# Four token tiles normalised on VectorE: a float32 transformer block on one Trainium2 core

## The chip, the core and the metric

The kernel runs on one core of a Trainium2 chip. The core has a matrix engine, TensorE (PE in the profile, with its weight loads as PEld), and three engines for everything else: VectorE (DVE), ScalarE (ACT) and GpSimd (POOL). SyncE (SP) issues the transfers between the chip's memory and the on-chip memory SBUF. Matmul results land in a second on-chip memory, PSUM. Each engine takes its instructions strictly in the order in which the program gives them, and waits at the first whose inputs are not ready. The metric is the device time of one execution in microseconds.

## The reference

One block of a transformer with two parallel branches on the same normalised input; 2048 tokens, width 576, all in float32:

```python
x = A_x
xn = _layernorm(x, axis=-1)          # (x - mean) / sqrt(var + 1e-5), over the 576 columns
return x + _A_ref(xn, A_wqkv, A_wo) + _B_ref(xn, B_w1, B_b1, B_w2)
```

`_A_ref` is attention with 32 heads of 18, where each token sees 8 earlier tokens at a distance of 2 from each other; `_B_ref` is a dense layer to 4608, the Mish function, and a dense layer back.

## The kernel before, in words

The tokens are worked through in two halves of 1024 (`hf` 0 and 1), each of two blocks of 512 (`b`), each of four tiles of 128 tokens (`jj`). A float32 number is split for TensorE into a high part, rounded to the format fp32r, and the low rest; a product is the sum of three matmuls (high by high, high by low, low by high). So every weight tile `wq_k` has a high half, made by a ScalarE cast, and a low half, made by a subtraction of the cast from the raw tile.

The program is one long list of items in the order of TensorE's work, and around each of them the code places the work of the other engines. The order on each engine is that of the code; a manual dependency on the instruction before fixes it. The list begins with `first_item(0)` to `first_item(3)`: the first group of query, key and value columns for the four tiles of the first block. `first_item(0)` runs `prologue()`, which normalises tiles 0 and 1. During the item of tile n, `mid()` is called between two of its 14 matmuls and transposes tile n + 1.

One tile goes through these steps:

- The load `acc_0_n` (SyncE, L59). The first tile, two weight tiles, the second tile and three weight tiles are loaded first; `hold` keeps the later loads back until the first tile's statistics are taken.
- `ln_stats`: two BN_STATS over 288 columns each (L114) and a BN_AGGR (L115) on VectorE give mean and variance, the two columns of `mv`.
- `ln_root`: VectorE adds epsilon to the variance (`ve`, L160), and ScalarE takes the inverse root by a logarithm and an exponential (`rs`, L161 and L162).
- `ln_newton`: VectorE makes the root exact with a Newton step (L169 to L171), and for ScalarE's use also computes `nm`, the negative product of mean and root (L172). Tiles 0 to 3 are each a group of their own (`k == 1`); tiles 4 and 5, and 6 and 7, are handled in pairs by the other branch.
- `ln_norm`: ScalarE writes `xn`, the tile times `rs` plus `nm` (L182), and GpSimd copies its last 64 columns once more behind it (L183).
- `ln_transpose`: GpSimd sets the rest aside (`rem`, L194); TensorE transposes the tile into the PSUM tiles `ta` and `tb` (L77, L78); ScalarE casts these to the high part of `xt` (L83 for `ta`, L88 for `tb`), and VectorE subtracts to get the low part (L84 for `ta`, L89 for `tb`). The matmuls of `qkv_item` (L349) read `xt` as their stationary operand.

`first_cast` makes the first five weight tiles: the high half on ScalarE at once (L1172), the low half (L1173, here always on GpSimd) when the function that it returns is called.

The core of `mid()` and its place among the matmuls, in short:

```python
if n == 0: ln_root(2); ln_newton(2)
ln_transpose(0, 0, n + 1)
if n == 0: ln_norm(2); ln_stats(3); ln_root(3); ln_newton(3)
if n == 1: ln_norm(3)
```

It stands before the twelfth matmul of tile 0, the ninth of tile 1 and the fifth of tile 2.

Of the kernel before, what the change touches and what calls it, by code (L numbers as in the profile page):

```python
# [10 lines left out]
AF = mybir.ActivationFunctionType  # L11
ALU = mybir.AluOpType
AX = mybir.AxisListType.X

S, D, F = 2048, 576, 4608
# [24 lines left out]
def block_kernel(ctx: ExitStack, tc: tile.TileContext, x, wq, wo, w1, b1, w2, mask, out):  # L40
    nc = tc.nc
# [11 lines left out]
    def load_x(hf, blocks=range(NB), jjs=range(JB)):  # L53
        tiles = []
        xv = x[hf * SH:(hf + 1) * SH, :].rearrange("(p j) d -> p j d", j=TJ)
        for b in blocks:
            for jj in jjs:
                t = sb.tile([P, D], F32, tag="acc", bufs=9, name=f"acc_{hf}_{b}_{jj}")
                nc.sync.dma_start(t, xv[:, b * JB + jj, :])  # L59
                tiles.append(t)  # L60
        return tiles
# [7 lines left out]
    def transpose_split(src, dst, col, extra=None, pair=False):  # L69
        n = next(tpn)  # L70
        if pair:
            ta, tb = (ps.tile([P, 512], F32, tag="out", bufs=4, name=f"tt{k}_{n}") for k in range(2))
        else:
            ta = ps.tile([P, 512], F32, tag="h", bufs=4, name=f"ta_{n}")
            tb = ps.tile([P, 512], F32, tag="h", bufs=4, name=f"tb_{n}")
        for k in range(KT):
            nc.tensor.transpose(ta[:, k * P:(k + 1) * P], src[:, k * P:(k + 1) * P], ident)  # L77
        nc.tensor.transpose(tb[:, 0:P], src[:, KT * P:(KT + 1) * P], ident)  # L78
        if extra is not None:
            nc.tensor.transpose(tb[:, P:2 * P], extra, ident)  # L80
        tav = ta.rearrange("p (k t) -> p k t", k=KT)
        hi = dst[:, 0:KT, col:col + P]
        nc.scalar.copy(hi, tav)  # L83
        nc.vector.tensor_sub(dst[:, 5:5 + KT, col:col + P], tav, hi.bitcast(F32))  # L84
        e = 1 if extra is None else 2
        hr = dst[:, KT:KT + 5 * e - 4:5, col:col + P]
        tbv = tb.rearrange("p (k t) -> p k t", k=KT)[:, 0:e]
        nc.scalar.copy(hr, tbv)  # L88
        nc.vector.tensor_sub(hr[64:P], tbv[64:P], hr[64:P].bitcast(F32))  # L89
# [20 lines left out]
    def stats(n, t, mv):  # L110
        st = odd.tile([P, 2, 6], F32, tag="st", bufs=4, name=f"st_{next(tpn)}")
        last = None
        for c in range(2):
            last = nc.vector.bn_stats(st[:, c, :], t[:, c * 288:(c + 1) * 288])  # L114
        nc.vector.bn_aggr(mv, st)  # L115
        return last

    def newton(rs, ve, y, eng=nc.vector):
        eng.tensor_mul(y, rs, rs)
        eng.tensor_mul(y, y, ve)  # L120
        eng.tensor_scalar(y, y, -0.5, 1.5, op0=ALU.mult, op1=ALU.add)
        eng.tensor_mul(rs, rs, y)
# [23 lines left out]
    def ln_group(ns):  # L146
        k = len(ns)
        mk_ = lambda w, c: odd.tile([P, 4, c], F32, tag=w, bufs=3, name=f"{w}_{ns[0]}")
        g = dict(n0=ns[0], k=k, mv=mk_("mv", 2), ve=mk_("ve", 1), rs=mk_("rs", 1), y=mk_("y2", 1), nm=mk_("nm", 1))
        for n in ns:  # L150
            group[n] = g

    def ln_stats(n):
        g = group[n]
        return stats(n, accs[0][n], g["mv"][:, n - g["n0"], :])

    def ln_root(n0):
        g = group[n0]
        k, rs, ve = g["k"], g["rs"][:, 0:g["k"]], g["ve"][:, 0:g["k"]]
        nc.vector.tensor_scalar_add(ve, g["mv"][:, 0:k, 1:2], EPS)  # L160
        nc.scalar.activation(rs, ve, AF.Ln)  # L161
        nc.scalar.activation(rs, rs, AF.Exp, scale=-0.5)  # L162

    def ln_newton(n0):
        g = group[n0]
        k, rs, ve, y, nm = g["k"], *(g[w][:, 0:g["k"]] for w in ("rs", "ve", "y", "nm"))
        if k == 1:
            r, v, y, m = rs[:, 0], ve[:, 0], y[:, 0], nm[:, 0]
            nc.vector.tensor_scalar(y, r, r, v, op0=ALU.mult, op1=ALU.mult)  # L169
            nc.vector.tensor_scalar(y, y, -0.5, 1.5, op0=ALU.mult, op1=ALU.add)  # L170
            nc.vector.tensor_scalar(r, r, y, None, op0=ALU.mult)  # L171
            nc.vector.tensor_scalar(m, g["mv"][:, 0, 0:1], r, -1.0, op0=ALU.mult, op1=ALU.mult)  # L172
        else:
            newton(rs, ve, y)
            nc.vector.tensor_mul(nm, g["mv"][:, 0:k, 0:1], rs)
            nc.vector.tensor_scalar(nm, nm, -1.0, None, op0=ALU.mult)

    def ln_norm(n):
        g = group[n]
        i = n - g["n0"]  # L180
        xn = sb.tile([P, 5 * P], F32, tag="xn", bufs=XNB, name=f"xn_0_{n}")
        nc.scalar.activation(xn[:, 0:D], accs[0][n], AF.Identity, bias=g["nm"][:, i, :], scale=g["rs"][:, i, :])  # L182
        nc.gpsimd.tensor_copy(xn[:, D:D + 64], xn[:, KT * P:D])  # L183
        xns[0, n] = xn

    def ln_transpose(hf, b, jj):
        if jj == 0:
            XTs[hf, b] = sb.tile([P, 9 + b, TB], F32R, tag=f"xt{b}", bufs=1, name=f"xt_{hf}_{b}")
        xn = xns[hf, b * JB + jj]
        if (b, jj) == (0, 0):  # L190
            rems[hf] = sb.tile([P, JB, P], F32, tag="tt", bufs=2, name=f"rem_{hf}")
        rem = rems[hf][:, jj, :]
        if b == 0:
            nc.gpsimd.tensor_copy(rem, xn[:, KT * P:])  # L194
        else:
            nc.gpsimd.tensor_tensor(out=rem, in0=rem, in1=xn[:, KT * P:], op=ALU.subtract)
        transpose_split(xn, XTs[hf, b], jj * P, rem if b else None, (hf, b) == (1, 0) and jj < 3)
# [21 lines left out]
    def new(kind, hf, i):  # L219
        tag, bufs, width = home(kind, i)  # L220
        return sb.tile([P, 2, width], F32R, tag=tag, bufs=bufs, name=f"{kind}_{hf}_{i}")
# [879 lines left out]
    accs = {0: load_x(0, [0], [0])}  # L1101
# [6 lines left out]
    def hold(ins):  # L1108
        tiles = load_x(0, [0], [2, 3])
        first = nc.cur_bb.bb.instructions[-len(tiles)]  # L1110
        tc.add_manual_dep(first, ins.ins.name,
                          mybir.DependencyInfo(mybir.DependencyClass.Sync, mybir.DependencyReason.DATA),
                          reason="the other tiles' loads begin behind the first tile's")
        for k in range(4):
            load("wq", 5 + k)
        accs[0].extend(tiles + load_x(0, [1]))
        rest_loads()
# [52 lines left out]
    def first_cast(k, eng):  # L1170
        t = done["wq", 0, k] = new("wq", 0, k)
        nc.scalar.copy(t[:, 0, :], rq0[k])  # L1172
        return lambda: eng.tensor_tensor(out=t[:, 1, :], in0=rq0[k], in1=t[:, 0, :].bitcast(F32),  # L1173
                                         op=ALU.subtract)

    def prologue():
        for ns in ((0,), (1,), (2,), (3,), (4, 5), (6, 7)):
            ln_group(ns)
        hold(ln_stats(0))
        ln_root(0)  # L1180
        first_cast(0, nc.gpsimd)()
        ln_newton(0)
        ln_stats(1)
        low1 = first_cast(1, nc.gpsimd)
        ln_norm(0)
        low1()
        first_cast(2, nc.gpsimd)()
        ln_root(1)
        ln_newton(1)
        ln_transpose(0, 0, 0)  # L1190
        first_cast(3, nc.gpsimd)()
        ln_norm(1)
        first_cast(4, nc.gpsimd)()
        ln_stats(2)

# [137 lines left out]
    def spot(hf, q, i):  # L1333
        return at["s", hf, q, i]

    for q in range(NP):
        if q == 0:
            i = at["q", 0, 3, 1, 0]
            ps_ = dict(raw=i - 3, sums=i - 1, wa=i, wc=i + 1, t0=i + 2, t1=i + 4)
        elif q == 1:  # L1340
            i = at["q", 0, 3, 0, 0]
# [16 lines left out]
    for q in range(1, 2 * OC + 1):  # L1358
        i = spot(0, q, (3,2)[q > 1])
# [5 lines left out]
    i = spot(0, NP - 1, 0)  # L1365
# [5 lines left out]
    i = at["q", 1, 0, 1, 1]  # L1371
# [4 lines left out]
    i = spot(0, 9, 4)  # L1376
# [10 lines left out]
    for q in range(NP):  # L1387
        if q == 0:
            i = at["z", JB - 1, 0]
            ps_ = dict(wa=i - 7, t0=i - 6, t1=i - 5, wc=i - 4)  # L1390
        elif q == 1:
            i = spot(1, 0, 0)
# [19 lines left out]
    for n, (a, b) in enumerate((("P6", "P1"), ("P7", "P6"), ("P6", "P5"), ("P2", "P1"), ("P3", "P6"), ("P4", "P7"), ("P5", "P7"))):  # L1412
        for pr in range(2):
            i = items[-2][2] + 1 + (0,1,2)[n] if n < 3 else at["p", 1, J + 0 - 1, n > 4, pr] + (1, 7, 1, 2)[n - 3]
# [6 lines left out]
    i = at["q", 0, 1, 1, 0]  # L1421
# [3 lines left out]
    i = at["q", 0, 3, 1, 0]  # L1425
# [5 lines left out]
    i = at["q", 1, 0, 1, 1]  # L1431
    for n in range(8):
        c, k = divmod(n, 4)
# [7 lines left out]
    for n in range(0, JB, 2):  # L1441
        i = at["q", 0, 1, 0, n]
# [4 lines left out]
    for n in range(TJ):  # L1447
        i = spot(0, 2 + n, 2)
# [3 lines left out]
    i = spot(0, NP - 2, 0)  # L1452
# [7 lines left out]
    for n, (name, pr) in enumerate((name, pr) for name in ("P4", "P5", "P2", "P3") for pr in range(2)):  # L1460
        i = items[dict(P4=0, P5=2, P3=2, P2=3)[name]][2] + pr
# [29 lines left out]
    k = marks[0] - 1  # L1491
    for n in range(2 * steps):
        t = n * total / (2 * steps)
        if n == steps:
            k = max(k, spot(1, 0, 0) + 1)
        k = next(k for k in range(k + 1, len(plan)) if T[k + 1] > t and ok[k])
# [6 lines left out]
    i = spot(1, *(11,3))  # L1503
# [4 lines left out]
    for n, name in enumerate(("T3", "T1", "T2", "T4", "B11", "B21", "B22", "R", "D")):  # L1508
        k = i + 10 + (0,5,10,15,20,25,30,35,40)[n]
# [5 lines left out]
    i = spot(1, NP - 1, 0)  # L1515
# [68 lines left out]
```

## Time and profile before

| | before |
|---|---|
| median of 3 runs | 1124.03 us (1123.45 to 1124.14) |
| span of the profiled execution | 1121.6 us |
| PE busy | 1109.5 us (99%) |
| VectorE busy | 829.0 us (74%) |
| ScalarE busy | 492.1 us (44%) |
| GpSimd busy | 787.7 us (70%) |

The span goes from the first instruction to the last on the core; the time of a run also has what lies around it. For the profiled execution the profile gives the span alone, 1121.6 us, which is 2.4 us below the median of the runs. A share of busy time is an average over all stages: the stretch that the change touches is the first 20 us.

### The profile page before, as it was taken

What the parts mean: (1) busy time and instruction counts of PE and PEld (TensorE: products, weight loads), DVE (VectorE), ACT (ScalarE), POOL (GpSimd) and SP (SyncE); (2) the same over time, 40 slices, a digit from 0 to 9 for tenths busy, and PEclk for the clock granted to TensorE, in tenths of its full rate; (3) what the DMA queues carried; (4) which work ended last, traced back from release to release, by engine and by line L of the source; (5) the groups of instructions that cost most, each with busy time, mean ns of one, the idle gap of its engine ahead of it and who ended that gap; (6) DMA issues with size and microseconds to landing.
All of it is one profiled execution on the core that took longest, in us unless ns stands there. A gap on an engine that the chain in (4) does not pass through costs nothing.

```text
span 1121.6 us, 18415 instructions
## 1 busy us (share of the span) xinstructions
PE 1109.5 (99%) x6630; PEld 1023.0 (91%) x6630; DVE 829.0 (74%) x1351; ACT 492.1 (44%) x892; POOL 787.7 (70%) x639
## 2 busy tenths in 40 slices
PE   8999999999999999999999999999999999999998
PEld 7999899999999999899999889999999999999998
DVE  6368788888888888877655456687866677776876
ACT  5544645544554545455233355343433343443332
POOL 2488767767689687676788476665789878668632
PEclk9999999999999999999999999999999999999999
DMA  6899885868767849666596797655655477676463
GB/s 200 283 312 318 290 283 205 289 228 284 261 240 258 282 163 345 222 240 214 191 342 238 231 373 249 241 200 174 227 198 189 168 263 269 215 253 248 157 222 104
DMA packets 147487, 271.08 MB, mean 242 GB/s; under 512 B 30114, under 2 KB 86724, under 8 KB 147396
## 3 DMA queue, kind: packets, MB, share of 16 engines
q1 hardware_dynamic: 147396, 269.91, 69.2%
q8 instruction: 52, 0.85, 0.3%
q14 instruction: 39, 0.32, 0.1%
HBM read 160.39 MB, written 109.48 MB: 241 GB/s over the span
## 4 chain that ended last, share of the span: by engine, by line
PE 89%; DVE 4%; POOL 3%; DMA 2%; issue 1%; ACT 1%; DVEq 0%; POOLq 0%; SPq 0%
PE h L657 28%; PE po L755 19%; PE pq L349 11%; PE po L868 10%; PE po L847 7%; PE h L663 5%; PE o L1056 4%; PE z L447 2%; DMA acc<-in_x 1%; POOL accP L856 1%; DVE u L801 1%; POOL pr L534 0%; DVE accP L871 0%; POOL act L709 0%; DMA z_B<-kept_wq 0%
## 5 line engine op out<-in xcount | busy, mean ns | idle before, releaser
L755 PEld LDWEIGHTS po<-w,act 128*128 128x128 f32 x1728 | 236.4, 188 | 7.5 <-DVE acc L759 1.7
L755 PE MATMUL po<-w,act 128*128 128x288 f32 x1728 | 240.8, 295 | 1.4 <-DVE acc L759 1.2
L534 POOL TENSOR_TENSOR pr<-q,kv 128x576 f32<-128x576 f32 x128 | 195.7, 1553 | 18.7 <-DMA q<-q_d 16.9
L572 POOL TENSOR_TENSOR pv<-L,kv 128x576 f32<-128x576 f32 x128 | 174.3, 1461 | 38.7 <-DVE L L565 20.9
L709 POOL TENSOR_TENSOR act<-c,act 128x512 fp32r<-128x512 f32 x81 | 107.1, 1322 | 128.4 <-ACT act L708 125.5
L759 DVE TENSOR_TENSOR acc<-po,acc 128x288 f32<-128x288 f32 x288 | 120.4, 450 | 31.6 <-PE po L755 30.2
L349 PE MATMUL pq<-wq,xt 128*128 128x432 f32 x672 | 136.2, 361 | 1.8 <-ACT xt L83 1.8
L868 PEld LDWEIGHTS po<-w,act 128*128 128x128 f32 x960 | 131.1, 188 | 3.7 <-DVE accP L871 0.4
L868 PE MATMUL po<-w,act 128*128 128x288 f32 x960 | 133.8, 295 | 0.2
L349 PEld LDWEIGHTS pq<-wq,xt 128*128 128x128 f32 x672 | 125.0, 188 | 8.7 <-ACT xt L83 2.7
L703 ACT ACTIVATE c<-c,b1c 128x512 f32<-128x512 f32 x81 | 58.7, 724 | 132.9 <-DVE c L702 132.6
L657 PE MATMUL h<-xt,t 128*128 128x512 f32 x432 | 110.6, 391 | 0.9 <-DVE c L702 0.8
L657 PE MATMUL h<-S,t 128*128 128x512 f32 x432 | 110.4, 391 | 0.0
L691 ACT COPY c<-h 128x512 f32<-128x512 f32 x81 | 47.4, 586 | 136.5 <-PE h L663 78.3
L578 DVE TENSOR_REDUCE og<-pv 128x144 f32<-128x1152 f32 x64 | 85.9, 1343 | 25.4 <-POOL pv L572 25.4
L657 PE MATMUL h<-xt,wa 128*128 128x512 f32 x432 | 104.0, 390 | 0.0
L657 PEld LDWEIGHTS h<-xt,wa 128*128 128x128 f32 x432 | 80.9, 188 | 16.9
L871 DVE TENSOR_TENSOR accP<-po,accP 128x288 f32<-128x288 f32 x160 | 69.6, 454 | 36.1 <-PE po L868 34.5
L847 PEld LDWEIGHTS po<-pw,u 128*128 128x128 f32 x672 | 92.4, 188 | 2.9 <-DVE u L801 0.5
L847 PE MATMUL po<-pw,u 128*128 128x288 f32 x672 | 94.2, 296 | 0.3 <-DVE u L801 0.3
L539 DVE TENSOR_REDUCE L<-pr 128x64 f32<-128x1152 f32 x64 | 85.8, 1341 | 11.2 <-POOL pr L534 11.1
L657 PEld LDWEIGHTS h<-xt,t 128*128 128x128 f32 x432 | 79.0, 188 | 16.1 <-DVE c L702 1.1
(231 smaller groups left out, 1840.5 us busy)
## 6 DMA issues: line engine op xcount, KB each, us to landing
kv<-kv_d SPq DMA_DIRECT2D x64, 396.0 KB, 5.2
kept_t<-t SPq DMA_DIRECT2D x36, 512.0 KB, 5.3
t<-kept_t SPq DMA_DIRECT2D x36, 512.0 KB, 5.4
rw<-in_w SPq DMA_DIRECT2D x36, 320.0 KB, 4.6
kept_wa<-wa SPq DMA_DIRECT2D x18, 640.0 KB, 3.5
kept_w<-w SPq DMA_DIRECT2D x20, 576.0 KB, 4.8
wa<-kept_wa SPq DMA_DIRECT2D x18, 640.0 KB, 6.1
w<-kept_w SPq DMA_DIRECT2D x20, 576.0 KB, 4.5
```

The lines of the kernel that those rows point to most:

```text
L349: nc.tensor.matmul(pq[:, 0:432], XT[:, xi, tok], wt[wi][:, hl, 0:432], start=i == 0, stop=i == len(seq) - 1)
L534: nc.gpsimd.tensor_tensor(out=pr[:, x:x + hh], in0=q[:, j0 + x:j0 + x + hh, None, :].to_broadcast([P, hh, W, CU]), in1=win(kt, 0, CU, j0 + ...
L539: nc.vector.tensor_reduce(L[:, k, j0:j0 + hj].rearrange("p j w h -> p (j w h)"), pr.rearrange("p j w (h d) -> p (j w h) d", h=2), axis=AX, ...
L572: nc.gpsimd.tensor_tensor(out=pr[:, x:x + hj].rearrange("p j d w -> p j w d"), in0=L[:, k, x:x + hj, :, h:h + 1].to_broadcast([P, hj, W, DH]),
L578: nc.vector.tensor_reduce(og[:, :, c0:c0 + DH], pr, axis=AX, op=ALU.add)
L657: nc.tensor.matmul(ph, wt[:, wl, wk * P:(wk + 1) * P], X[:, xs, :], start=first and i == 0, stop=last and i == len(seq) - 1, skip_group_ch ...
L709: nc.gpsimd.tensor_tensor(out=a[:, 1, :], in0=t, in1=a[:, 0, :].bitcast(F32), op=ALU.subtract)
L755: nc.tensor.matmul(po, acts[hf, q, b, j][:, al, tok], done["w2", hf, 2 * q + j][:, wl, c * HC:(c + 1) * HC], start=i == 0, stop=i == 5)
L759: nc.vector.tensor_tensor(out=t, in0=po, in1=t, op=ALU.add)
L847: nc.tensor.matmul(po, units[e, k, qq][:, al, tok], w[:, qq, wl, :], start=i == 0, stop=i == 5)
L868: nc.tensor.matmul(po, acts[hf, q, b, j][:, al, tok], done["w2", hf, 2 * q + j][:, wl, c * HC:(c + 1) * HC], start=i == 0, stop=i == 5)
L871: nc.vector.tensor_tensor(out=t, in0=po, in1=t, op=ALU.add)
```

## The change

For tiles 0 to 3 (`k == 1`) the normalisation is one VectorE instruction, (tile − mean) times root, in place of ScalarE's. The instruction that computed `nm` for them is gone. In the prologue tile 0 is normalised ahead of tile 1's statistics, and tile 1 ahead of the transposes of tile 0; the casts stay in their order among themselves. Tiles 4 to 7 and the second half keep ScalarE's form.

```diff
@@ ln_newton
         if k == 1:
-            r, v, y, m = rs[:, 0], ve[:, 0], y[:, 0], nm[:, 0]
+            r, v, y = rs[:, 0], ve[:, 0], y[:, 0]
             nc.vector.tensor_scalar(y, r, r, v, op0=ALU.mult, op1=ALU.mult)
             nc.vector.tensor_scalar(y, y, -0.5, 1.5, op0=ALU.mult, op1=ALU.add)
             nc.vector.tensor_scalar(r, r, y, None, op0=ALU.mult)
-            nc.vector.tensor_scalar(m, g["mv"][:, 0, 0:1], r, -1.0, op0=ALU.mult, op1=ALU.mult)
@@ ln_norm
-        nc.scalar.activation(xn[:, 0:D], accs[0][n], AF.Identity, bias=g["nm"][:, i, :], scale=g["rs"][:, i, :])
+        if g["k"] == 1:
+            nc.vector.tensor_scalar(xn[:, 0:D], accs[0][n], g["mv"][:, i, 0:1], g["rs"][:, i, :], op0=ALU.subtract, op1=ALU.mult)
+        else:
+            nc.scalar.activation(xn[:, 0:D], accs[0][n], AF.Identity, bias=g["nm"][:, i, :], scale=g["rs"][:, i, :])
         nc.gpsimd.tensor_copy(xn[:, D:D + 64], xn[:, KT * P:D])
@@ prologue
         ln_newton(0)
+        ln_norm(0)
         ln_stats(1)
-        low1 = first_cast(1, nc.gpsimd)
-        ln_norm(0)
-        low1()
+        first_cast(1, nc.gpsimd)()
         first_cast(2, nc.gpsimd)()
         ln_root(1)
         ln_newton(1)
+        ln_norm(1)
         ln_transpose(0, 0, 0)
         first_cast(3, nc.gpsimd)()
-        ln_norm(1)
         first_cast(4, nc.gpsimd)()
```

How the instructions stand on an engine is shown at three places. A row gives the line, the operation, the written tile and the read ones, with numbers behind the names that only tell buffers apart; the line numbers of the changed kernel are one to two higher. The first place is VectorE at tile 0 (`acc_0_0`), from its Newton step to the statistics of tile 1 (`acc_0_1`). Before:

```order
L169 TENSOR_SCALAR y_0_144<-rs_143,ve_142 128x1
L170 TENSOR_SCALAR y_0_144<-y_0_144 128x1
L171 TENSOR_SCALAR rs_143<-rs_143,y_0_144 128x1
L172 TENSOR_SCALAR nm_145<-mv_141,rs_143 128x1
L114 BN_STATS st_211<-acc_0_1_121 128x6 x2
L115 BN_AGGR mv_146<-st_211 128x2
```

With the change, at the same place:

```order
L169 TENSOR_SCALAR y_0_144<-rs_143,ve_142 128x1
L170 TENSOR_SCALAR y_0_144<-y_0_144 128x1
L171 TENSOR_SCALAR rs_143<-rs_143,y_0_144 128x1
L182 TENSOR_SCALAR xn_0_210<-acc_0_0_117,mv_141,rs_143 128x576
L114 BN_STATS st_213<-acc_0_1_121 128x6 x2
L115 BN_AGGR mv_146<-st_213 128x2
```

The instruction of one column for `nm` is replaced by one of 576 columns that writes `xn_0`. At tile 1 the same happens ahead of L84 of tile 0.

The second place is VectorE during the item of tile 0: the Newton step of tile 2, the low parts of tile 1's transposes (`ta`, `tb`), and the statistics of tile 3 (`acc_0_3`). Before:

```order
L169 TENSOR_SCALAR y_2_154<-rs_153,ve_152 128x1
L170 TENSOR_SCALAR y_2_154<-y_2_154 128x1
L171 TENSOR_SCALAR rs_153<-rs_153,y_2_154 128x1
L172 TENSOR_SCALAR nm_155<-mv_151,rs_153 128x1
L84 TENSOR_TENSOR xt_0_231<-ta_280,xt_0_231 128x4x128
L89 TENSOR_TENSOR xt_0_231<-tb_281,xt_0_231 64x128
L114 BN_STATS st_294<-acc_0_3_177 128x6 x2
L115 BN_AGGR mv_156<-st_294 128x2
```

With the change:

```order
L169 TENSOR_SCALAR y_2_154<-rs_153,ve_152 128x1
L170 TENSOR_SCALAR y_2_154<-y_2_154 128x1
L171 TENSOR_SCALAR rs_153<-rs_153,y_2_154 128x1
L84 TENSOR_TENSOR xt_0_232<-ta_277,xt_0_232 128x4x128
L89 TENSOR_TENSOR xt_0_232<-tb_278,xt_0_232 64x128
L182 TENSOR_SCALAR xn_2_288<-acc_0_2_175,mv_151,rs_153 128x576
L114 BN_STATS st_291<-acc_0_3_177 128x6 x2
L115 BN_AGGR mv_156<-st_291 128x2
```

`nm` is gone from ahead of L84, and the normalisation of tile 2 stands behind L89 and ahead of tile 3's statistics. For tile 3 it is alike: its normalisation stands behind L84 and L89 of tile 2.

The third place is GpSimd, from the low half of the first weight tile on; `xn_0` and `xn_1` name the copies of the last columns. Before:

```order
L1173 TENSOR_TENSOR wq_0_204<-rq_0_112,wq_0_204 128x432
L183 COPY xn_0_217<-xn_0_217 128x64
L1173 TENSOR_TENSOR wq_1_215<-rq_1_113,wq_1_215 128x432
L1173 TENSOR_TENSOR wq_2_221<-rq_2_114,wq_2_221 128x432
L194 COPY rem_232<-xn_0_217 128x128
L1173 TENSOR_TENSOR wq_3_245<-rq_3_115,wq_3_245 128x432
L183 COPY xn_1_248<-xn_1_248 128x64
L1173 TENSOR_TENSOR wq_4_251<-rq_4_116,wq_4_251 128x432
```

With the change:

```order
L1175 TENSOR_TENSOR wq_0_204<-rq_0_112,wq_0_204 128x432
L185 COPY xn_0_210<-xn_0_210 128x64
L1175 TENSOR_TENSOR wq_1_217<-rq_1_113,wq_1_217 128x432
L1175 TENSOR_TENSOR wq_2_220<-rq_2_114,wq_2_220 128x432
L185 COPY xn_1_229<-xn_1_229 128x64
L196 COPY rem_233<-xn_0_210 128x128
L1175 TENSOR_TENSOR wq_3_246<-rq_3_115,wq_3_246 128x432
L1175 TENSOR_TENSOR wq_4_249<-rq_4_116,wq_4_249 128x432
```

The copy for tile 1 moved ahead of `rem` of tile 0 and of the low half of `wq_3`.

## Rows read from the trace of the kernel before

**Rows 1.** Busy time by stretch of the span (columns in the first line)

```profile
core 0: us, PE busy (x) PEld busy (x) DVE busy (x) ACT busy (x) POOL busy (x), PEclk, DMA share, GB/s
18.28:32.00 13.72, 13.72 (x74) 13.10 (x74) 8.79 (x28) 6.72 (x20) 1.23 (x4) 1.00 0.58 202
32.00:1121.60 1089.60, 1081.58 (x6483) 997.78 (x6480) 808.75 (x1285) 474.29 (x846) 778.95 (x618) 1.00 0.70 242
```

**Rows 2.** Timeline of PE and its weight loads: start, duration, instruction, idle time before

```profile
7.46 0.66 PE L77 MATMUL ta<-ident,xn 128*128 128x128 f32 x4 [0.91 <-ACT xn L182]
...
9.34 2.45 PE L349 MATMUL pq<-wq,xt 128*128 128x432 f32 x11 [1.11 <-ACT xt L83]
...
17.29 1.05 PE L349 MATMUL pq<-wq,xt 128*128 128x432 f32 x4 [0.65 <-ACT xt L83]
...
18.28 0.42 PEld L77 LDWEIGHTS ta<-ident,xn 128*128 128x128 f32 x4 [0.30 <-ACT xn L182]
```

**Rows 3.** Timeline of ScalarE

```profile
6.55 0.87 ACT L182 ACTIVATE xn<-acc,nm,rs 128x576 f32<-128x576 f32 x1 [0.18 <-ACT wq L1172]
...
8.61 0.20 ACT L162 ACTIVATE rs<-rs 128x1 f32<-128x1 f32 x1
8.72 0.57 ACT L83 CAST xt<-ta 128x512 fp32r<-128x512 f32 x1
...
12.39 0.57 ACT L83 CAST xt<-ta 128x512 fp32r<-128x512 f32 x1
...
16.64 0.60 ACT L83 CAST xt<-ta 128x512 fp32r<-128x512 f32 x1
...
17.36 0.87 ACT L182 ACTIVATE xn<-acc,nm,rs 128x576 f32<-128x576 f32 x1
```

**Rows 4.** Timeline of VectorE

```profile
0.88 0.48 DVE L1122 MEMSET zeros<- 8x504 f32 x1 [0.88 <-PEq L1573]
...
5.50 0.27 DVE L169 TENSOR_SCALAR y<-rs,ve 128x1 f32<-128x1 f32 x1 [0.50 <-ACT rs L162]
5.80 0.15 DVE L170 TENSOR_SCALAR y<-y 128x1 f32<-128x1 f32 x1
5.99 0.21 DVE L171 TENSOR_SCALAR rs<-rs,y 128x1 f32<-128x1 f32 x1
6.24 0.21 DVE L172 TENSOR_SCALAR nm<-mv,rs 128x1 f32<-128x1 f32 x1
7.09 0.82 DVE L114 BATCH_NORM_STATS2 st<-acc 128x6 f32<-128x288 f32 x2 [0.64 <-DMA acc<-in_x]
...
9.59 0.22 DVE L172 TENSOR_SCALAR nm<-mv,rs 128x1 f32<-128x1 f32 x1
9.72 0.68 DVE L84 TENSOR_TENSOR xt<-ta,xt 128x512 fp32r<-128x512 f32 x1
...
13.51 0.69 DVE L84 TENSOR_TENSOR xt<-ta,xt 128x512 fp32r<-128x512 f32 x1
14.23 0.30 DVE L89 TENSOR_TENSOR xt<-tb,xt 64x128 fp32r<-64x128 f32 x1
14.56 0.82 DVE L114 BATCH_NORM_STATS2 st<-acc 128x6 f32<-128x288 f32 x2
```

**Rows 5.** Timelines of VectorE and GpSimd from 48 to 53 us

```profile
48.77 1.29 POOL L608 TENSOR_TENSOR s<-xt,s 128x512 f32<-128x512 f32 x1
...
49.56 0.96 DVE L257 TENSOR_TENSOR wq<-rwq,wq 128x432 fp32r<-128x432 f32 x1 [2.02 <-ACT wq L256]
...
52.33 0.61 DVE L257 TENSOR_TENSOR wq<-rwq,wq 128x432 fp32r<-128x432 f32 x1 [1.80 <-ACT wq L256]
```

**Rows 6.** One line's instructions (L313): count, durations in ns (min/median/max)

```profile
L313 DVE TENSOR_TENSOR twT<-twT,twhT x16: 745/752/1847, 131.6 to 299.3; 128x576 fp32r<-128x576 f32 x16
```

**Rows 7.** Timeline of GpSimd, low halves of the first and last weight tile

```profile
5.99 1.09 POOL L1173 TENSOR_TENSOR wq<-rq,wq 128x432 fp32r<-128x432 f32 x1 [4.70 <-ACT wq L1172]
...
11.29 1.12 POOL L1173 TENSOR_TENSOR wq<-rq,wq 128x432 fp32r<-128x432 f32 x1
```

## The prediction

> **What bounds the kernel now.** I read the busy table by stretches first. From 18.28 us to 32.00 us TensorE (PE) is busy for all 13.72 us, and from 32.00 us to the end for 1081.58 of 1089.60 us [rows 1]. So behind 18.28 us PE is the bound, with 8.0 us of gaps in all, and a delay ahead of that point can only be made up out of those gaps. All that the change touches lies ahead of it. There I read PE's timeline for its waits: 1.11 us before the first projection matmul at 9.34, on L83 of tile 0; 0.65 us before tile 2's first matmul at 17.29, on L83 of tile 2; 0.30 us at 18.28 before the transposes of tile 3, on the normalisation L182 of tile 3 [rows 2]. Then I followed each of the three waits back through ScalarE and VectorE.
>
> ScalarE's L83 of tile 0 starts at 8.72, as soon as the exponential of tile 1 at 8.61 is through [rows 3]; the transposes that it reads had been begun at 7.46, so L83 waits for its turn in the queue and not for its input. The same holds for tiles 1 and 2 (L83 at 12.39 and 16.64): ahead of each stands the root of the next tile, and that root waits for the next tile's statistics on VectorE. VectorE's timeline shows where these come from: tile 1's statistics start at 7.09 when the load of the tile lands; tile 3's start at 14.56, right behind L89 of tile 1 [rows 4]. From tile 1's root on VectorE waits for nothing but the roots, so the chain statistics, root, Newton, L84, L89, next statistics sets the pace of tiles 1 to 3. ScalarE is not the limit; its 0.87 us normalisations lie beside VectorE's work.
>
> **What the change does, part by part.** Call n the length of the new VectorE instruction on a 128x576 tile.
>
> Removed: four L182 on ScalarE (0.87 us each) and four nm on VectorE (0.21 us each; 0.25 us from one start to that of the next, as from 5.99 to 6.24) [rows 3, 4]. Added: four instructions of n on VectorE, in the chain just found.
>
> What is n? No row of before has it. Three rows of one element show what the scalars cost: 0.15 us with constants (L170), 0.21 us with one scalar from a tile (L171), 0.27 us with two (L169) [rows 4]. The new instruction has two, so 0.27 us is the bound from below. Two SBUF tensors are subtracted in 0.61 us at 432 elements and in 0.745 us at 576 [rows 5, 6]: 0.94 ns an element. At that rate 576 elements after 0.27 us give 0.27 + 0.54 = 0.81 us; adding the two scalars' 0.12 us to the 0.745 us gives 0.87 us, the bound from above. But the new instruction reads one tensor, not two, and the one row of VectorE without a second tensor of this length, the memset of 504 elements, took 0.48 us in all [rows 4], of which 0.94 ns an element would need 0.47 us for the elements alone, with nothing for the 0.15 us that even a one-element instruction takes. So instructions with fewer streams can run faster than one element per 0.94 ns. I take two elements in that time: n = 0.27 + 0.27 = 0.54, say 0.55 us, and keep 0.27 and 0.87 us for the range.
>
> The Trainium skill says as much ("VectorE: DVE Perf Modes", section "The perf-mode tier table"): a float32 tensor_scalar within SBUF runs at twice the base rate, 1227 ns for 2048 elements. With the page's 0.96 GHz and its fixed cost of some 150 cycles an estimate is (288 + 150) / 0.96 = 0.46 us for n; the sum below would then be +1.1 us in place of +1.4. No row of before shows such an instruction.
>
> There is a second cost. A VectorE subtraction of two SBUF tensors that began at 49.56, while GpSimd's instruction of 48.77 ran until 50.06, took 0.96 us in place of 0.61: it ended 0.46 us behind GpSimd's end, the time that its elements need [rows 5]. It waited for GpSimd and then streamed. The new instruction for tile 0 would begin at 6.25 (where nm began), inside GpSimd's L1173 of 5.99 to 7.08 [rows 7]. If it takes both read paths to stream two elements at a time, it waits as well and ends at 7.08 + 0.27 + 0.05 = 7.40; if not, at 6.25 + 0.55 = 6.80.
>
> The skill speaks here against the change ("SBUF — State Buffer", section "Who interferes with whom"): a tensor_scalar in a two-port mode and GpSimd exclude each other for a whole instruction, and whichever issued first goes on. The rows of the two-tensor subtraction agree, 0.96 against 0.61 us; for the new form no run here shows it yet.
>
> Now the path, tile by tile, in times of before.
>
> Tile 0: xn_0 is there at 7.40 or 6.80 in place of 7.42. Either way this is worth nothing, since L83 stands behind the root of tile 1, and that behind tile 1's load at 7.09. The moved statistics are hidden by this load as long as the normalisation is over by then. With the wait for GpSimd it isn't: independent VectorE instructions overlap by 0.09 us (nm 9.59 to 9.81, L84 at 9.72), so the statistics start at 7.40 − 0.09 = 7.31. Call this shift a: +0.22 us, or 0 without the wait. I take 0.22.
>
> Tile 1: n stands in place of nm ahead of L84 of tile 0: +0.55 − 0.21 = +0.34. L84 comes at 9.72 + 0.22 + 0.34 = 10.28, the statistics of tile 2 are 0.56 late, and with them its root and L83 of tile 1: 12.39 becomes 12.95. That xn_1 comes off ScalarE earlier is worth nothing: PE works through tile 0 at that time.
>
> Tile 2: no nm between Newton and L84, −0.25: L84 of tile 1 goes from 13.51 to 13.82 and L89 from 14.23 to 14.54, with its end at 14.84. In before ScalarE normalised tile 2 beside these two; now the normalisation stands behind them, 14.87 to 15.42, and tile 3's statistics, until now at 14.56, start at 15.33: +0.77. Its root and L83 of tile 2 follow: 16.64 becomes 17.41, and PE's tile 2 starts at 18.06 in place of 17.29.
>
> Tile 3: L84 of tile 2 waits for L83's end (17.41 + 0.60) and starts at 18.05; L89 ends at 19.06; the normalisation runs from 19.09 to 19.64; the transposes of tile 3 load at 19.69 in place of 18.28. In before ScalarE did this at 17.36, right behind L88, and did not have to let L84 and L89 by.
>
> Sum: 19.69 − 18.28 = **+1.4 us**; as a formula a + 3n − 0.48. With n = 0.27 and a = 0 it is +0.3; with n = 0.87, a = 0, +2.1; with 0.87 and the wait (a grows by the 0.32 us that n grew, to 0.54) +2.7. The formula changes sign at n = 0.16, below the 0.27 us of one element, so within my bounds there is no gain on this path.
>
> Two moves cost nothing. The first casts and their order on ScalarE: the cast of wq_2 is fixed by its load. On GpSimd the copy for xn_1 now stands ahead of rem of tile 0 and of the low halves of wq_3 and wq_4, and holds them until tile 1 is normalised: xn_1 is there at 9.59 + 0.22 + 0.55 = 10.36, and with two short copies and twice 1.12 us the last of them, 11.29 to 12.41 in before [rows 7], ends near 13.1. PE's last matmul of tile 0 wants it; but the next one, tile 1's first, waits for L83 until 12.95 + 0.57 = 13.52 anyway. Without this cover PE would wait the 0.7 us from 12.41 to 13.1.
>
> Behind 18.28 the delay stays, as PE has no gap until 32.00 and every later queue hangs on PE's items.
>
> The profiled execution's span is 1121.6 us; with the sum it is 1123.0. The median of before is 1124.03, 2.4 us more, for what lies around the span, which the change leaves alone. 1124.03 + 1.4 = **1125.4 us**. That is 0.12%, inside the 0.2% (2.2 us) that a measurement of this kernel can tell from no change.
>
> **The rivals.**
> - *One element at a time.* The new instruction takes 0.81 to 0.87 us. For it: all float32 rows with two tensors run at this rate. Against: the memset. It gives +2.0 to +2.1, with the wait for GpSimd +2.7: 1126.1 to 1126.7. The point from which it counts as slower is 3n + a > 2.7, as with 0.87 us and a wait of 0.12 us.
> - *Short instruction, or delay absorbed.* At n = 0.35 without the wait the sum is +0.6; or the 8.0 us of later gaps take back a part. 1124.0 to 1124.7, no change.
> - *Faster, by other meetings.* Later VectorE subtractions meet GpSimd's instructions and last 0.96 for 0.61 us; a shift of 1.4 us deals these meetings anew, and PE's 8.0 us of gaps behind 32.00 may shrink. To gain at all it must give back over 1.4 of the 8.0 us, to count as faster 3.6: 1121.8. Against: everything there hangs on the same PE items, so the engines shift together and meet as before.
>
> **How the numbers follow.** Forecast case (n 0.4 to 0.65, with or without the wait, +0.7 to +1.7) 0.54; one element at a time 0.26, of which 0.11 comes out over 2.2 us; short or absorbed 0.11; other meetings 0.05; that a longer prologue costs more than worked out, for instance at the later joins, 0.04, slower. Slower by over 0.2%: 0.11 + 0.04 = 0.15, and 0.01 for a median that is noisy upward: 0.16. Faster 0.05. Same 0.79. The range runs from the sum's lower bound to its upper one, each widened by half of the spread of the runs of before (0.69 us): 1124.03 + 0.3 − 0.35 = 1124.0 and 1124.03 + 2.7 + 0.35 = 1127.1.
>
> **What would show it.** In the profile after, VectorE's L182 lasts near 0.55 us (first one 1.15, ending with GpSimd's instruction, if it waits); tile 1's statistics start near 7.3; tile 3's near 15.3; PE's tile 2 starts near 18.1 and the transposes of tile 3 near 19.7, with no PE gap then until about 33.4. The forecast is wrong if L83 of tile 0 comes earlier than 8.72, if the transposes of tile 3 come before 18.28, if the granted clock, 1.00 in both stretches, falls in the longer waits of PE, or if PE's busy time behind the prologue no longer fits its stretch.

## The result, and the profile after

The changed kernel takes 1125.95 us (median of 21 runs, 1125.06 to 1127.24), the kernel before 1124.03 (21 runs, 1122.72 to 1125.55): a ratio of 1.0016, 95% interval 1.001 to 1.0023. It is slower by about 1.9 us, with the interval from 1.1 to 2.6 us. The forecast was 1125.4 us. A change of under 0.2%, which the prediction had put below what a measurement can tell from no change, is told from it by 21 runs of each kernel. The profiled execution of the changed kernel has a span of 1124.3 us.

VectorE's timeline of the changed kernel, to be laid beside [rows 4]:

```profile
6.19 1.17 DVE L182 TENSOR_SCALAR xn<-acc,mv,rs 128x576 f32<-128x576 f32 x1
7.27 0.81 DVE L114 BATCH_NORM_STATS2 st<-acc 128x6 f32<-128x288 f32 x2
...
9.76 0.58 DVE L182 TENSOR_SCALAR xn<-acc,mv,rs 128x576 f32<-128x576 f32 x1
10.26 0.68 DVE L84 TENSOR_TENSOR xt<-ta,xt 128x512 fp32r<-128x512 f32 x1
...
14.52 0.29 DVE L89 TENSOR_TENSOR xt<-tb,xt 64x128 fp32r<-64x128 f32 x1
14.85 0.58 DVE L182 TENSOR_SCALAR xn<-acc,mv,rs 128x576 f32<-128x576 f32 x1
15.34 0.81 DVE L114 BATCH_NORM_STATS2 st<-acc 128x6 f32<-128x288 f32 x2
...
18.04 0.69 DVE L84 TENSOR_TENSOR xt<-ta,xt 128x512 fp32r<-128x512 f32 x1 [0.24 <-ACT xt L83]
18.76 0.29 DVE L89 TENSOR_TENSOR xt<-tb,xt 64x128 fp32r<-64x128 f32 x1
19.09 0.58 DVE L182 TENSOR_SCALAR xn<-acc,mv,rs 128x576 f32<-128x576 f32 x1
```

The new instruction lasts 0.58 us three times and 1.17 us the first time. GpSimd's timeline of the same kernel shows what it met there:

```profile
5.93 1.10 POOL L1175 TENSOR_TENSOR wq<-rq,wq 128x432 fp32r<-128x432 f32 x1 [4.65 <-ACT wq L1174]
```

GpSimd is through at 7.03, the normalisation ends 0.33 us behind it, and the statistics of tile 1 (7.27) no longer start with their load but with the normalisation's end. In ScalarE's and PE's timelines the answers to [rows 2, 3] are:

```profile
8.78 0.20 ACT L162 ACTIVATE rs<-rs 128x1 f32<-128x1 f32 x1
8.89 0.57 ACT L83 CAST xt<-ta 128x512 fp32r<-128x512 f32 x1
...
17.41 0.60 ACT L83 CAST xt<-ta 128x512 fp32r<-128x512 f32 x1
```

```profile
7.41 0.66 PE L77 MATMUL ta<-ident,xn 128*128 128x128 f32 x4
...
9.51 2.73 PE L351 MATMUL pq<-wq,xt 128*128 128x432 f32 x11 [1.33 <-ACT xt L83]
...
18.06 1.04 PE L351 MATMUL pq<-wq,xt 128*128 128x432 f32 x4 [0.56 <-ACT xt L83]
19.81 0.63 PE L77 MATMUL ta<-ident,xn 128*128 128x128 f32 x4 [0.71 <-DVE xn L182]
```

Tile 0 is transposed at 7.41, as before, and its L83 still stands behind the root of tile 1. Tile 2's matmuls start 0.77 us later than in [rows 2]. Tile 3's transposes start 1.52 us later, with a new wait of 0.71 us on VectorE's L182. The row at 18.28 in [rows 2] is that of the weight load; PE's own row of before is this, and has no wait:

```profile
18.29 0.65 PE L77 MATMUL ta<-ident,xn 128*128 128x128 f32 x4
```

From there I compared PE's matmuls one by one, the same 6630 in both profiles: the changed kernel's lag stays between 1.5 and 1.7 us up to 658 us, and at 670 us it goes to 2.67 us, and stays between 2.6 and 2.7 us to the end. So 1.6 of the 2.7 us between the two spans come from the prologue, and 1.1 us from one place in the middle. The spans differ by more than the medians because the profiled execution of before was one of its shorter ones: every run whose span is known took 1.7 to 1.9 us more than its span, so that this one took about 1123.4 us, 0.6 us under the median, and that of the changed kernel took 1126.1 us.

### The profile page after: what moved, and what is told of

Read it like the earlier page. It is cut to its first block, busy times and chain, and to the rows that moved or that the text cites. A ratio compares the mean times of both kernels' runs of the same rounds, so it can differ in the third digit from the quotient of the medians.

```text
span 1124.3 us, 18406 instructions
## 1 busy us (share of the span) xinstructions
PE 1111.0 (99%) x6630; PEld 1024.1 (91%) x6630; DVE 829.9 (74%) x1351; ACT 488.7 (43%) x888; POOL 789.4 (70%) x639
## 4 chain that ended last, share of the span: by engine, by line
PE 87%; DVE 5%; POOL 2%; DMA 2%; issue 2%; ACT 1%; SPq 0%; DVEq 0%; POOLq 0%; ACTq 0%
PE h L659 28%; PE po L757 19%; PE pq L351 11%; PE po L870 10%; PE po L849 6%; PE h L665 5%; PE o L1058 4%; PE z L449 2%; POOL pr L536 1%; DMA wo<-wkept_B 1%; POOL accP L858 1%; DVE u L803 1%; DVE accP L855 1%; DMA z_B<-kept_wq 0%; PE ta L77 0%
```

## The experiments

The reading of all of them is one distance: from the start of tile 1's statistics on VectorE to the start of tile 3's transposes on PE. The first of these times moves from execution to execution where the second tile's load sets it, so the distance is what the program makes. It leaves out what the change does ahead of its first end: the shift of tile 1's statistics itself, 7.27 for 7.09 in the first profiles.

| kernel | tile 1's statistics | tile 3's transposes | distance | time, ratio to before (95%) |
|---|---|---|---|---|
| before | 7.09 | 18.29 | 11.20 | |
| before again | 6.93 | 18.13 | 11.20 | 0.9998 (0.9989 to 1.0008) |
| changed | 7.27 | 19.81 | 12.54 | 1.0016 (1.001 to 1.0023) |
| changed again | 7.37 | 19.93 | 12.56 | 1.0022 (1.0012 to 1.0031) |
| e1, tiles 0 and 1 | 7.21 | 18.75 | 11.54 | 1.0006 (0.9997 to 1.0015) |
| e2, tiles 2 and 3 | 6.69 | 18.89 | 12.20 | 1.001 (1.0001 to 1.0018) |
| e3, cast early | 7.50 | 20.07 | 12.57 | 1.0015 (1.0006 to 1.0024) |
| c1, the same again | 7.31 | 20.50 | 13.19 | 1.0011 (1.0002 to 1.002) |
| e4, tile 3 first | 7.26 | 18.93 | 11.67 | 1.0006 (0.9998 to 1.0015) |
| b3, given twice | 7.89 | 22.29 | 14.40 | 1.004 (1.0025 to 1.0055) |
| b4, tile 3 alone | 6.82 | 17.91 | 11.09 | 0.9997 (0.9988 to 1.0007) |
| c2, statistics early | 7.35 | 17.92 | 10.57 | 0.9994 (0.9985 to 1.0002) |

**e1 and e2: one half of the tiles at a time.** In e1 `ln_norm` takes VectorE for tiles 0 and 1, in e2 for tiles 2 and 3; the other two keep `nm` and ScalarE, and e2 has the prologue's order of before. The lines for both are left out here.

```diff
-        if g["k"] == 1:
+        if n < 2:            # e1;  e2: n in (2, 3)
             nc.vector.tensor_scalar(xn[:, 0:D], accs[0][n], ...)
```

> Tiles 0 and 1 on VectorE as in the change, tiles 2 and 3 on ScalarE with nm as before. The delay is read as the start of PE's transposes of tile 3 against 18.29 us of before (19.82 with the change, +1.5). Theory, the delay is added where the new instruction stands in VectorE's chain: the first normalisation waits for GpSimd (+0.2), the second stands for nm ahead of L84 (+0.4), nothing more behind: +0.55 at tile 3, and about +0.5 us in the time. Rival, the moved statistics of tile 1 and the prologue's order make the loss: all of +1.5 is here already.

> Tiles 2 and 3 on VectorE as in the change, tiles 0 and 1 on ScalarE with nm and the prologue's order as before. Theory: tile 2's instruction, 0.58 us long, less the nm that is gone, delays tile 3's statistics by 0.25, and tile 3's stands behind L84 and L89 (+0.7): the transposes of tile 3 at 19.25, +0.95, and about +1 us in the time. Rival, the prologue's order makes the loss: 18.29 and no change.

The distance grows by 0.34 us in e1 and by 1.00 us in e2; together 1.34, and the whole change has 1.34 (12.54 − 11.20). So the parts add up, three quarters of this loss are tiles 2 and 3, and the rival is out: with the prologue's order of the change e1 has 0.46 us at tile 3's transposes (18.75 for 18.29), not 1.5. In the times e1 cannot be told from before, and e2 only just; together they come to the 1.0016 of the whole change. In the absolute times e2 looks better than expected, 18.89 for 19.25, since its load landed 0.4 us earlier.

**e3 and c1: GpSimd out of the way.** The cast of wq_0 goes ahead of tile 0's root, so that GpSimd's subtraction is over when the first normalisation begins.

```diff
-        ln_root(0)
         first_cast(0, nc.gpsimd)()
+        ln_root(0)
```

> The change, with the cast of wq_0 ahead of tile 0's root on ScalarE, so that GpSimd's low half of wq_0 runs about 4.9 to 6.0 and is over when the first normalisation begins at 6.2. Theory, that instruction waited for GpSimd: it lasts 0.58 us in place of 1.17, tile 1's statistics start when their load lands (7.1), and the transposes of tile 3 start 0.2 us sooner than with the change, +1.3 against before. Rival, the first one lasts 1.17 us for another reason (a first use, the loads that land then): still 1.17 us and +1.5.

VectorE's timeline of e3:

```profile
6.08 0.58 DVE L182 TENSOR_SCALAR xn<-acc,mv,rs 128x576 f32<-128x576 f32 x1
7.50 0.82 DVE L114 BATCH_NORM_STATS2 st<-acc 128x6 f32<-128x288 f32 x2 [0.85 <-DMA acc<-in_x]
```

The first one falls to 0.58 us: it had waited for GpSimd. But the load landed at 7.50 in this execution, so the start that was set free gained nothing, and the transposes came at 20.07, where 1.3 us over before (19.59) had been expected. The second run was meant to tell the landing from a fixed time:

> The kernel of e3_cast_early once more: there the first new instruction fell to 0.58 us, but the second tile's load landed 0.4 us later than in the profile of before and hid the gain. Theory, that load sets when tile 1's statistics start once the wait for GpSimd is gone: they start at the landing, and the transposes of tile 3 come 12.6 us behind that start (7.50 and 20.07 in the first run). Rival, the statistics start at a time of their own: 7.5 again whatever the landing.

The statistics started at 7.31 and so follow the load, but the distance was not 12.6 but 13.19 us: this expectation failed. The windows of c1 show why (columns as in [rows 1]; the last but two is the granted clock):

```profile
9.50:11.20 1.70, 1.63 (x7) 1.13 (x8) 1.60 (x5) 1.08 (x4) 0.82 (x4) 1.00 1.06 394
11.20:14.80 3.60, 3.60 (x13) 3.31 (x14) 2.26 (x9) 1.16 (x4) 2.10 (x3) 0.53 0.99 373
14.80:18.70 3.90, 3.51 (x20) 2.99 (x19) 2.98 (x10) 1.37 (x6) 0.54 (x2) 1.00 0.02 8
```

From 11.2 to 14.8 us PE was granted about half of its clock, near the lower level of 1.2 GHz, and did 13 matmuls there; e3 did 19 in the same stretch at a granted clock of 1.00. In c1 PE had stood idle for 1.95 us ahead of its first matmul at 9.56, because tile 0's transposes were done early and the next work was not. In e3 it had stood idle for 2.16 us, and the clock stayed. Nor does the idle time by itself tell the two cases apart: in b3 PE stood idle for 1.52 us ahead of tile 0's transposes and for 1.33 us behind them, and its clock stayed at 1.00, while c1 had another 0.47 us ahead of the transposes. So the clock can fall after such waits and doesn't each time, and why it fell in this execution stays open. Of the distance the lower clock took 0.6 us (13.19 − 12.57). This execution was the slowest of c1's ten (1127.36 us, median 1125.61). No time shows a gain from the freed wait: 1.0015 and 1.0011 here, 1.0016 and 1.0022 with the wait.

**e4 and b4: another place for tile 3.** In e4 the changed kernel normalises tile 3 ahead of L84 and L89 of tile 2. b4 is the kernel before with that alone: tile 3 on VectorE at this place, tiles 0 to 2 on ScalarE.

```diff
         def mid():
...
+            if n == 1:
+                ln_norm(3)
             ln_transpose(0, 0, n + 1)
...
-            if n == 1:
-                ln_norm(3)
```

> The change, with tile 3's normalisation ahead of L84 and L89 of tile 2 on VectorE, where that engine waits for L83. Theory, the place makes most of tile 3's part: it runs near 17.85 to 18.45, PE goes from tile 2's fourth matmul to the transposes without a wait at about 18.9, +0.6 against before in place of +1.5, and the time gains about 0.9 us on the change. Rival, the instruction costs the same wherever it stands in the queue: +1.5 stays.

> The kernel before with tile 3 alone normalised on VectorE, ahead of L84 and L89 of tile 2, where that engine waits for L83, and without nm for it. Theory: it begins where nm began, at 17.07, ends at 17.65, and L84 of tile 2 follows 0.35 us late, which its matmuls still cover; the transposes of tile 3 start when PE is through with tile 2's fourth matmul, 18.14 in place of 18.29, and the time is that of before. Rival, that the new instruction costs its length wherever it stands: +0.4 to +0.6.

VectorE's and then PE's timeline of e4:

```profile
17.82 0.58 DVE L182 TENSOR_SCALAR xn<-acc,mv,rs 128x576 f32<-128x576 f32 x1
```

```profile
18.93 0.60 PE L77 MATMUL ta<-ident,xn 128*128 128x128 f32 x4
```

The same instruction of 0.58 us now begins in VectorE's wait for L83, which is 0.24 us long in the changed kernel, and pushes L84 from 18.04 to 18.43; PE, busy with tile 2's matmuls and tile 3's transposes, does not wait for that. It goes into the transposes without a wait, and the distance falls from 12.54 to 11.67: 0.87 of the 1.34 us was the place of one instruction. In b4 the distance is 11.09, 0.1 us under that of before, and the time the same as before. The rival, that the instruction costs its length anywhere, is out by the distances; the times point the same way (1.0006 for e4, 1.0016 for the change), with intervals that overlap.

**b3: each new instruction twice.**

```diff
-            nc.vector.tensor_scalar(xn[:, 0:D], ...)
+            for _ in range(2):
+                nc.vector.tensor_scalar(xn[:, 0:D], ...)
```

> The change with each of the four new instructions given twice. Theory, all four are on VectorE's chain: two independent instructions overlap by 0.09, so a copy adds 0.5 us, four add 2.0 us: the transposes of tile 3 at 21.8, +3.5 against before. If the copy waits for the first one, 0.6 each and +3.9. Rival, VectorE has idle time there and hides them: +1.5 stays, or about half of the rise.

VectorE's timeline of b3, tiles 1 to 3:

```profile
10.38 1.19 DVE L183 TENSOR_SCALAR xn<-acc,mv,rs 128x576 f32<-128x576 f32 x2
...
16.08 1.20 DVE L183 TENSOR_SCALAR xn<-acc,mv,rs 128x576 f32<-128x576 f32 x2
...
20.94 1.20 DVE L183 TENSOR_SCALAR xn<-acc,mv,rs 128x576 f32<-128x576 f32 x2
```

The copy does not overlap the first one, so each of these pairs lasts 1.2 us, as in the second branch of the expectation. The transposes of tile 3 come at 22.29, 4.0 us behind those of before; the distance grows by 1.85 us on the changed kernel, 0.62 for each of tiles 1 to 3, and tile 1's statistics by 0.62 as well. So every lengthening arrives in full at PE; for the first of the four this holds once its end is behind the load's landing, as it is here. The time follows: 1.004.

**b1 and b2: both kernels again.** For what one kernel's executions differ by.

> The kernel before, once more, for how far two executions of one kernel differ at the two places where all the profiles of changed kernels differ from that of before: the landing of the second tile's load (6.7 to 7.5 us so far), and PE's wait of 1.1 us for L702 at 670 us, which stood in five profiles of changed kernels and not in the one of before. Theory, that wait is drawn anew in each execution by when a load lands, and is no part of the change: it may stand here too, and the time is that of before. Rival, the shift of 0.5 to 1.8 us brings it about: it is not here, and the profile repeats that of before within 0.2 us.

> The changed kernel once more. Theory: the four new instructions last 1.17 (or less, as far as GpSimd's instruction is over) and 0.58 us, and the transposes of tile 3 are 1.4 to 1.6 us later than 18.29 once the landing of the second tile's load is taken out. The wait of 1.1 us at 672 us may stand or not. Rival for that wait, that the shift brings it about: it is here again.

The distances repeat within 0.02 us. The wait in the middle turned up in the kernel before as well, with 0.93 us. Against this second profile, a span of 1122.4 us, those of the changed kernel, 1124.3 and 1124.4 us, are 1.9 and 2.0 us longer: with the wait on both sides the difference is that of the medians. The timeline of the changed kernel there (GpSimd, VectorE, PE; other rows left out):

```profile
670.87 1.43 POOL L835 TENSOR_TENSOR accP<-accP,accP 128x576 f32<-128x576 f32 x1 [0.55 <-DMA accP<-in_x]
671.11 1.47 DVE L557 TENSOR_TENSOR L<-L,m 128x256 f32<-128x256 f32 x1
672.50 0.68 DVE L704 TENSOR_TENSOR rt<-h,rt 128x512 f32<-128x512 f32 x1
...
673.24 0.74 PE L659 MATMUL h<-xt,t 128*128 128x512 f32 x2 [1.07 <-DVE rt L704]
```

and that of the kernel before in its second profile, at the same place:

```profile
669.03 1.43 POOL L833 TENSOR_TENSOR accP<-accP,accP 128x576 f32<-128x576 f32 x1 [0.41 <-DMA accP<-in_x]
669.41 1.33 DVE L555 TENSOR_TENSOR L<-L,m 128x256 f32<-128x256 f32 x1
670.66 0.68 DVE L702 TENSOR_TENSOR rt<-h,rt 128x512 f32<-128x512 f32 x1
...
671.39 1.42 PE L657 MATMUL h<-xt,t 128*128 128x512 f32 x5 [0.93 <-DVE rt L702]
```

A load releases GpSimd's addition. When it lands just ahead of VectorE's subtraction of two SBUF tensors (L555, L557 after), VectorE waits, and PE with it, here for 1.1 and 0.9 us; in the first profile of before GpSimd began 0.15 us behind VectorE, L555 took 0.43 us, and PE had no wait. The shift is not needed for it. Whether it makes it more frequent stays open: the wait of 0.7 to 1.3 us stands in one of the two profiles of before and in nine of the ten of the other kernels. In those ten GpSimd's addition began ahead of VectorE's subtraction, and in the other two, the first of before and b4, behind it. Another wait, 1.2 us at 911 to 913 us, stands in b4 and e1.

**c2: tile 3's statistics earlier.** b4, with the statistics of tile 3 in VectorE's wait for tile 2's root.

```diff
             if n == 0:
                 ln_root(2)
+                ln_stats(3)
                 ln_newton(2)
...
                 ln_norm(2)
-                ln_stats(3)
                 ln_root(3)
```

> The kernel of b4_only_norm3, with tile 3's statistics ahead of tile 2's Newton step on VectorE, in its wait for tile 2's root. Theory, the chain statistics, root, Newton, L84, L89, next statistics sets the pace: with the statistics taken out of it the root of tile 3 no longer holds L83 of tile 2 back, and though tile 2's normalisation comes 0.6 us later, PE's transposes of tile 3 start 0.3 to 0.5 us sooner than in the kernel before, counted from the landing of the second tile's load. In the time that is too little to be told from no change. Rival, tile 2's later normalisation holds PE as long: no gain or a loss.

PE's timeline of c2:

```profile
15.81 2.22 PE L353 MATMUL pq<-wq,xt 128*128 128x432 f32 x10
17.92 0.66 PE L77 MATMUL ta<-ident,xn 128*128 128x128 f32 x4
```

PE no longer waits for L83 of tile 2, and the distance is 10.57, 0.63 us under before; 0.3 to 0.5 us had been expected. The span is not shorter than the first one of before (1122.4 for 1121.6 us): the load landed later, and the wait in the middle stands here. The median is 1123.26 us against 1123.96 for before on the same chip, a ratio of 0.9994 whose interval reaches to 1.0002: against before it can't be told from no change. Its interval lies wholly below those of the changed kernel.

## Why the prediction was right, point by point

- **What bounds.** VectorE's chain in the prologue sets PE's start on each tile, and PE keeps the delay: shown by b3, where 0.62 us more in each instruction gave 0.62 us at each tile, and by the lag of 1.5 to 1.7 us that stands up to 658 us. One of the three waits was misread: the 0.30 us at 18.28 are idle time of the weight loads, and PE itself had none there, so ScalarE's normalisation of tile 3 held back next to nothing in before; b4, which takes it away, gained 0.11 us.
- **The length n.** I took 0.55 us; it is 0.58, so it streams faster than one element in 0.94 ns behind its 0.27 us, which would have been 0.81 us. The rival with one element at a time is out. The estimate that the prediction made from the Trainium skill ("VectorE: DVE Perf Modes", section "The perf-mode tier table"), 0.46 us, is too short. Its double rate fits: behind the 0.27 us of one element the 576 elements took 0.31 us, 0.54 ns each, against 0.94 ns for two tensors. The fixed cost taken with it does not hold here; the 0.12 us that it lacks are what the rows of one element have more with two scalars from tiles (0.27 us) than with constants (0.15 us). Both are read from one length, so this split is argued and not shown.
- **The wait for GpSimd.** Forecast end 7.40, measured 7.36, and gone in e3. The Trainium skill ("SBUF — State Buffer", section "Who interferes with whom") says that such an instruction in a two-port mode and GpSimd shut each other out for a whole instruction, and the trace agrees: 1.17 us with GpSimd at work, 0.58 without. Its price was the uncertain part: 0.18 us against the load's landing at 7.09 in the first profile of before, close to the forecast 0.22. That is in part luck: the landing goes from 6.69 to 7.50 us in these profiles, with a late one the wait costs nothing, and e3 and c1, without it, showed no gain in time.
- **Tile by tile.** Tile 3's statistics: forecast 15.33, measured 15.34. PE's tile 2: 18.06, measured 18.06. The load of tile 3's transposes: 19.69, measured 19.78, and on PE +1.52 us for a forecast of +1.4; tile 3's normalisation started at 19.09, as forecast (up to there a longer n and a shorter wait for GpSimd nearly cancelled), and the rest is its length and the step from its end to the load, 0.11 us for 0.05. The part of tiles 2 and 3 was 1.00 of 1.34 us in e2.
- **The moves at no cost.** GpSimd's copy for tile 1 did hold back the low halves of wq_3 and wq_4 to 13.02, as forecast (13.1); PE's weight load waited 0.26 us for the last one and then another 0.29 us for L83, so L83 still ended the wait.
- **What was too small.** The measured change is +1.9 us, the forecast +1.4. The prologue gives 1.5 to 1.7 us; the rest lies within the interval (1.1 to 2.6 us) and may be the wait at 670 us, which I had taken as meeting as before. That part is not settled. The 2.4 us between the span and the median of before were misread as what lies around the span: that is 1.7 to 1.9 us, and the rest is that the profiled execution was a short one. The forecast was counted from the median, so this did not touch it. The rival of other meetings, which was to make the kernel faster, has the right mechanism with the wrong sign in this profile.

## What to carry to other kernels

In this kernel an instruction moved to a "faster" engine cost its full length where that engine's queue was the chain, and nothing where the queue waited and PE covered the rest: the same 0.58 us cost 0.87 us more behind L89 than ahead of L84, where b4 shows no cost against the kernel before. Before a move, mark in the timeline where the receiving engine waits, what stands behind the new place, and which GpSimd instruction runs beside it. And before counting a result that comes earlier, look at what its reader stands behind: tile 0, transposed 0.5 us sooner in e3 than in the changed kernel (6.88 for 7.41), gave PE only a longer wait (2.16 for 1.33 us).

## What the runs showed of the hardware that I had not expected

With tile 0 transposed early PE stood idle 1.95 us and then ran from 11.2 to 14.8 us at a granted clock of 0.53 in one execution (c1), while after 2.16 us of idle time the clock stayed at 1.00 in another execution of the same kernel (e3). The landing of one early load of 288 KB moved between 6.69 and 7.50 us over executions of kernels that issue it alike, and a single meeting of GpSimd and VectorE in the middle of the kernel made PE wait for 0.7 to 1.3 us, of which the first profile of the changed kernel kept 1.1 us to the end.
